# Seven products in place of eight in two stages of a chain of matrix products on one core

## The chip, the core and the metric

The kernel runs on one core of a Trainium2 chip. The time is that of one execution on the device, in us; less is better.

## What is computed

Three stages follow each other, all in float32 at the borders. Attention with a decay makes `x` (1536 tokens by 512), a gated product of two linear maps makes `y`, and a softmax-like stage with a normalisation makes the output:

```python
attn_out = _attn_ref(**attn_kwargs)                  # 16 heads, 12 blocks of 128 here, a carried state
x = np.ascontiguousarray(attn_out.transpose(0, 2, 1, 3)).reshape(B * S, H * D)
...
a = x @ w_a                                          # 1536 x 512 by 512 x 1536
b = x @ w_b
x = (a * b @ w_out).astype(np.float32)               # by 1536 x 512
...
h = x @ w_in                                         # 1536 x 512 by 512 x 1024
h_max = np.max(h, axis=-1, keepdims=True)
e = np.exp(h - h_max)
sm = e / (np.sum(e, axis=-1, keepdims=True) + 1e-09)
solu = h * sm
mu = np.mean(solu, axis=-1, keepdims=True)
var = np.mean((solu - mu) ** 2, axis=-1, keepdims=True)
ln = (solu - mu) / np.sqrt(var + 1e-06) * g_ln
return (ln @ w_out).astype(np.float32)               # by 1024 x 512
```

## The kernel before

Each factor of a large product is scaled by a power of two and split into a high and a low half in float16; `mm3` then makes each product of two tiles from three matmuls (high by high, high by low, low by high), accumulated in one PSUM bank of 512 float32 columns. There are eight banks, taken by `bank`.

The tokens are worked in 12 chunks `n` of 128 (two batches in turn, six blocks each) and in three groups `t` of 512. For each chunk, `scores`, `products` and `carry` do the attention in float32 with small matmuls, `kdecay`, `qdecay` and `fade` prepare operands on GpSimd; `scale_x` finds a scale and `split_x` writes the two halves of `x`. Weights come in as 1 MB pieces: `load_w` on the DMA queue of SP, `decode` (two ScalarE passes, a VectorE shift, a maximum), `scale_w` (through `spread` and `pow2`, which send a maximum over partitions through TensorE), `split_w`.

`L1(t, f)` makes 128 rows of `a` and of `b` for a group `t`: 12 matmuls each into `pa` and `pb`, then ScalarE copies `pa`, VectorE multiplies by `pb`, ScalarE casts to the high half and GpSimd subtracts for the low one (`g`). `f` runs over 12 blocks, so there are 36 calls. `L2(t, d)` multiplies by `w_out` over all 12 `f` in four quarters of 12 matmuls; `scale_y` and `split_y` split `y`. `L3(t, j)` makes `h` of one chunk in two banks `ph` (24 matmuls of 512 columns) and carries on to the softmax and the normalisation; `Z` splits and transposes the result, `L4` is the last product and sends it out.

All these are generators. ORDER is a list of words such as `L,0,3`, written out by hand or by a planner: each word runs its generator up to its next `yield`, so ORDER alone sets the order of instructions on every engine's queue, each of which works in order. SBUF tiles come from fixed numbers of buffers by kind (`BUFS`: 6, 11, 18 of 4 KB a partition, 3 of 8 KB, and others); a tile waits until an earlier one of its kind is released. The constants `lam`, `dec` and `gl` are loaded from GpSimd's queue at the start.

Of the kernel before, what the change touches and what calls it, by code (L numbers as in the profile page):

```python
# [587 lines left out]
```

## Time and profile before

| | us |
|---|---|
| median of three runs (lowest to highest) | 474.37 (473.40 to 475.82) |
| the profiled execution | 473.23 |
| its span | 471.5 |
| TensorE busy with matmuls | 455.6 (2682 of them) |
| weight loads, beside the matmuls | 230.8 |
| VectorE busy | 281.3 |
| ScalarE busy | 185.1 |
| GpSimd busy | 125.2 |

Busy time counts every us in which an engine has an instruction in work. The profile names the engines PE (TensorE; PEld its weight loads), DVE (VectorE), ACT (ScalarE), POOL (GpSimd) and SP (the one that issues DMA). Matmul records overlap, so the cost of one in a stream is its distance from the next, not its duration. A number after L is a line of the kernel before.

### The profile page before, as it was taken

Reading aid. Unit: us, or ns where it says so; the run is one execution under the profiler, and the core shown is the slowest. Engines: PE = TensorE matmul, PEld = TensorE weight load, DVE = VectorE, ACT = ScalarE, POOL = GpSimd, SP = SyncE. Lnnn points to the kernel's source line nnn. Section 1 sums busy time; section 2 is a strip of 40 time slices with the busy share of each in tenths; the row PEclk is TensorE's granted clock in tenths of the full one; section 3 lists DMA queues with packets and bytes.
Section 4 is the critical chain, followed back from the end, with each engine's and each line's share of the span. In section 5 each row is a group of like instructions: output and inputs, shape, how many; then the busy total and the mean of one; then the engine's idle time right before and its main releaser. Section 6 shows DMA issues by size and latency. Waiting matters only on the chain.

```text
span 471.5 us, 6724 instructions
## 1 busy us (share of the span) xinstructions
PE 455.6 (97%) x2682; PEld 230.8 (49%) x2682; DVE 281.3 (60%) x529; ACT 185.1 (39%) x289; POOL 125.2 (27%) x183
## 2 busy tenths in 40 slices
PE   3899999999999999999999999999999999999997
...
GB/s 272 414 207 181 267 180 0 2 91 245 201 188 179 170 178 90 178 89 91 1 2 89 90 0 0 1 0 1 45 2 22 23 111 83 74 128 30 68 89 46
DMA packets 30320, 48.69 MB, mean 103 GB/s; under 512 B 22224, under 2 KB 22480, under 8 KB 26960
## 3 DMA queue, kind: packets, MB, share of 16 engines
...
## 4 chain that ended last, share of the span: by engine, by line
PE 87%; DVE 8%; DMA 2%; issue 1%; POOL 1%; ACT 0%; DVEq 0%; POOLq 0%
PE py L128 20%; PE pb L128 18%; PE pa L128 17%; PE po L128 13%; PE ph L128 13%; PE px L225 2%; DMA dec<-in_dec_dram 2%; DVE fab L289 2%; PE pss L204 2%; DVE st_ab L102 1%; PE px L220 1%; DVE sc L209 1%; DVE xh L267 1%; DVE wab L343 1%; DVE xst L102 1%
## 5 line engine op out<-in xcount | busy, mean ns | idle before, releaser
L128 PEld LDWEIGHTS <-wab 128*128 128x128 f16 x888 | 85.7, 98 | 98.5 <-DVE wab L343 1.3
L128 PE MATMUL pa<-xh,wab 128*128 128x512 f16 (+1 forms) x444 | 98.5, 373 | 1.1 <-DVE wab L343 0.8
L373 POOL TENSOR_TENSOR g<-asb,g 128x512 f16<-128x512 f32 x36 | 46.7, 1310 | 196.9 <-ACT g L371 196.8
L128 PE MATMUL pb<-xh,wab 128*128 128x512 f16 (+1 forms) x444 | 98.4, 373 | 0.0
L128 PE MATMUL py<-g,wo 128*128 128x512 f16 x432 | 94.3, 379 | 0.0
L128 PEld LDWEIGHTS <-wo 128*128 128x128 f16 x432 | 42.2, 98 | 50.6
L366 DVE TENSOR_TENSOR asb<-asb,pb 128x512 f32<-128x512 f32 x36 | 24.4, 684 | 67.2 <-PE pb L128 62.8
L128 PE MATMUL po<-wo,zT 128*128 128x512 f16 (+1 forms) x312 | 63.4, 363 | 0.0
L128 PE MATMUL ph<-wi,yh 128*128 128x512 f16 x288 | 63.4, 379 | 0.0
L128 PEld LDWEIGHTS <-zT 128*128 128x128 f16 x312 | 30.5, 98 | 31.5
L128 PEld LDWEIGHTS <-yh 128*128 128x128 f16 x288 | 28.1, 98 | 33.7
L364 ACT ACTIVATE asb<-pa 128x512 f32<-128x512 f32 x36 | 20.8, 590 | 53.2 <-PE pa L128 48.8
L371 ACT CAST g<-asb 128x512 f16<-128x512 f32 x36 | 21.3, 614 | 26.5 <-DVE asb L366 26.5
L287 ACT ACTIVATE raw<-raw 128x1024 f32<-128x1024 f32 x26 | 29.5, 1136 | 0.0
L477 POOL TENSOR_TENSOR zr<-e,zr 128x512 f16<-128x512 f32 x20 | 22.7, 1156 | 23.0 <-ACT zr L473 23.0
L102 DVE TENSOR_REDUCE ym<-py 128x1 f32<-128x512 f32 x12 | 8.3, 691 | 31.4 <-PE py L128 31.3
L437 ACT ACTIVATE e<-ph,st,ch 128x512 f32<-128x512 f32 x24 | 18.4, 776 | 19.0 <-DVE st L432 13.7
L518 ACT ACTIVATE ob<-po,glm 128x512 f32<-128x512 f32 (+1 forms) x13 | 8.5, 655 | 41.7 <-PE po L128 41.7
L430 DVE TENSOR_REDUCE st<-ph 128x1 f32<-128x512 f32 x24 | 15.9, 674 | 12.9 <-PE ph L128 12.8
L473 ACT CAST zr<-e 128x512 f16<-128x512 f32 x20 | 11.4, 618 | 28.0 <-DVE e L462 28.0
L204 PE MATMUL pss<-qk 64*128 64x128 f32 x192 | 15.3, 308 | 7.1 <-DMA qk<-in_qk_dram 7.1
L340 ACT ACTIVATE wab<-fab,sab 128x512 f16<-128x512 f32 x24 | 15.9, 714 | 16.0 <-DVE sab L122 15.7
(109 smaller groups left out, 462.9 us busy)
## 6 DMA issues: line engine op xcount, KB each, us to landing
...
zT<-zr SPq DMA_TRANSPOSE x20, 3.1
...
```

The costliest lines, as they stand in the source:

```text
L102: nc.vector.tensor_reduce(out=dst, in_=src, axis=AX.X, op=ALU.max, apply_absolute_value=True)
L128: nc.tensor.matmul(o, w[a], x[b], start=start and i == 0, stop=stop and i == 2, skip_group_check=True)
L204: nc.tensor.matmul(pss[e][:, a * P:(a + 1) * P], t[r, 1, a], t[r, 0, a], start=True, stop=True, skip_group_check=True)
L287: nc.scalar.activation(hi.bitcast(F32), hi.bitcast(F32), AF.Prelu, scale=2.0 ** -112, alpha=2.0 ** 32)
L340: nc.scalar.activation(w[:, z, 0], src[:, z], AF.Copy, scale=s)
L364: nc.scalar.activation(a, pp[0], AF.Copy, scale=2.0 ** -63)
L366: nc.vector.tensor_mul(a, a, pp[1])
L371: nc.scalar.copy(g[:, 0], a)
L373: nc.gpsimd.tensor_sub(g[:, 1], a, g[:, 0])
L430: nc.vector.tensor_reduce(out=st[:, z:z + 1], in_=ph[z], axis=AX.X, op=ALU.max)
L437: nc.scalar.activation(e[z], ph[z], AF.Exp, bias=st[:, 2:3], scale=c, accum_out=st[:, 3 + z:4 + z])
L477: nc.gpsimd.tensor_sub(lo, e[z], hi)
```

## The change

Two products are made by a scheme of Strassen's kind (Winograd's form, with seven block products and fifteen sums in place of eight block products):

- `x w_a` and `x w_b` for pairs 2 to 5 of the blocks `f` and all three groups `t`: `R1(t, p)` takes the place of two `L1`. The blocks are two halves of the 512 inputs, two blocks `f`, and two halves of the 512 tokens, so its matmuls have 256 columns. Pairs 0 and 1 stay with `L1`.
- `y w_in` for all chunks: `L3(t, i)` makes two chunks at once, with matmuls of 512 columns. What followed in `L3` is now `norm(t, j)`; for the even chunk it works on 1024 columns in SBUF at once.

The sums of blocks are made by `sums_x`, `sums_w`, `sums_y`, `sums_i`, and split into halves by `sums_x` itself, `split_s`, `split_ys`, `split_si`. Weights `a` and `b` share one scale for two `f`; scales leave two more bits of room (TOP). `pow2` keeps its maximum in PSUM and the reciprocal of a scale is taken later (`turn`). One kind of 41 buffers takes the place of four kinds, `lam`, `dec` and `gl` are loaded from ScalarE's queue, and ORDER is written anew (1322 words in place of 1050).

```diff
-ORDER = ("G,qk,0 G,kv,0 G,qk,1 G,ab,0 G,kv,1 G,qk,2 G,kv,2 G,qk,3 G,kv,3 G,ab,1 G,qk,4 G,kv,4 G,qk,5 G,kv,5 A,0 K,0 A,1 K,0 A,0 T,0 A,1 T,0 A,1 O,2 A,0 D,ab,0 "
+ORDER = ("G,qk,0 G,qk,1 G,qk,6 G,kv,0 G,kv,1 G,qk,3 G,qk,2 G,ab,2 G,kv,3 G,ab,1 G,kv,2 G,kv,4 G,kv,7 G,qk,5 A,0 A,1 A,0 A,0 Q,6 A,6 A,1 K,0 C,0 A,1 K,0 A,6 C,1 "
...
-BUFS = {"in": 6, "w": 11, "g": 18, "xy": 3, "raw": 2, "row": 8}
+PLAIN, PLAINW = [0, 1, 2], [0, 1]
+TOP = 12
+BUFS = {"k": 41, "raw": 2, "row": 8}
...
-        m = sm.tile([P, n], F32, name=f"m{n}")
+        m = pm[:, n * P:n * P + n]
...
-    nc.gpsimd.dma_start(out=lam8, in_=lam)
+    nc.scalar.dma_start(out=lam8, in_=lam)
     dec = const.tile([P, NP, P], F32, name="dec")
-    nc.gpsimd.dma_start(out=dec[:, :, 0:1], in_=dec0)
+    nc.scalar.dma_start(out=dec[:, :, 0:1], in_=dec0)
...
+    def sums_x(m):
+        t, i = m // 2, m % 2
+        s1, s2 = sx[m][:, 0, :1], sx[m][:, 0, 1:]
+        o1, o2 = (px[n].rearrange("p (a i) -> p a i", a=NP) for n in (2 * m, 2 * m + 1))
+        b12 = t_row("b12", (P, 2, P))
+        tt = t_k("tt", (P, 4, 2, P))
+        nc.scalar.activation(b12, o2[:, :2], AF.Copy, scale=s2)
+        yield
+        for k, (a, s, op, b) in enumerate(((o1[:, :2], s1, ALU.subtract, b12), (o2[:, 2:], s2, ALU.add, tt[:, 0]), (o2[:, 2:], s2, ALU.subtract, b12), (o1[:, 2:], s1, ALU.subtract, tt[:, 1]))):
+            nc.vector.scalar_tensor_tensor(out=tt[:, k], in0=a, scalar=s, in1=b, op0=ALU.mult, op1=op)
+            yield
+        if t not in xt:
+            xt[t] = [t_k("xt", (P, 2, 2, W), F16) for _ in range(2)]
+        hl = [[xt[t][k][:, :, z].rearrange("p a (q i c) -> p q a i c", q=2, i=2)[:, :, :, i] for z in range(2)] for k in range(2)]
+        for k in range(2):
+            nc.scalar.copy(hl[k][0], tt[:, 2 * k:2 * k + 2])
+            yield
+        for k in range(2):
+            nc.gpsimd.tensor_sub(hl[k][1], tt[:, 2 * k:2 * k + 2], hl[k][0])
...
+    def sums_w(p):
+        def w(e, k):
+            return fw["ab", 2 * p + e][:, :, k * W // 2:(k + 1) * W // 2]
+        fs[p] = [t_k("s12", (P, 2, W))]
+        u = [fs[p][0][:, :, k * W // 2:(k + 1) * W // 2] for k in range(2)]
+        nc.gpsimd.tensor_add(u[0], w(1, 0), w(1, 1))
+        yield
+        nc.gpsimd.tensor_sub(u[1], u[0], w(0, 0))
+        yield
+        fs[p].append(t_k("s34", (P, 2, W)))
+        v = [fs[p][1][:, :, k * W // 2:(k + 1) * W // 2] for k in range(2)]
+        nc.gpsimd.tensor_sub(v[0], w(0, 0), w(1, 0))
+        yield
+        nc.gpsimd.tensor_sub(v[1], u[1], w(0, 1))
...
+    def split_s(p, k):
+        src = fs[p][k]
+        w = wt["s", p, k] = t_k("ws", (P, 2, 2, W), F16)
+        ss = sab[:, 0, p]
+        for z in range(2):
+            nc.scalar.activation(w[:, z, 0], src[:, z], AF.Copy, scale=ss[:, z:z + 1])
...
+    def R1(t, p):
+        x = xs[t]
+        H = W // 2
+        f, h = (lambda z, e=e: wt["ab", 4 * p + 2 * e + z] for e in range(2))
+        u, v = (lambda z, k=k: wt["s", p, k][:, z] for k in range(2))
+        def product(o, w, k, x, i, start, stop):
+            for z in range(2):
+                for kk in range(2):
+                    ks = slice((2 * k + kk) * P, (2 * k + kk + 1) * P)
+                    mm3(o[:, z], (w(z)[:, 0, ks], w(z)[:, 1, ks]), (x[:, kk, 0, i * H:(i + 1) * H], x[:, kk, 1, i * H:(i + 1) * H]), start and z == 0 and kk == 0, stop and z == 1 and kk == 1)
+        def acc(nm):
+            return bank(nm).rearrange("p (z n) -> p z n", z=2)
+        def kept(nm, o):
+            r = t_row(nm, (P, 2, H))
+            nc.scalar.activation(r, o, AF.Copy, scale=2.0 ** -28)
+            return r
+        A, Bk = acc("rA"), acc("rB")
+        product(A, f, 0, x[0], 0, True, False)
+        yield
+        product(Bk, u, 0, xt[t][0], 0, True, False)
+        yield
+        p1 = kept("p1", A)
+        yield
+        product(A, u, 1, xt[t][0], 1, False, False)
+        yield
+        p5 = kept("p5", Bk)
+        yield
+        product(Bk, v, 1, x[1], 1, False, True)
+        yield
+        p16 = kept("p16", A)
+        yield
+        product(A, v, 0, xt[t][1], 0, False, False)
+        yield
+        c0 = t_k("c0", (P, 2, 2, H))
+        nc.vector.scalar_tensor_tensor(out=c0[:, 1], in0=Bk, scalar=-2.0 ** -28, in1=p16, op0=ALU.mult, op1=ALU.add)
+        yield
+        C = acc("rC")
+        product(C, f, 1, x[1], 0, True, True)
+        yield
+        p167 = kept("p167", A)
+        yield
+        product(A, h, 1, xt[t][1], 1, False, True)
+        yield
+        nc.vector.scalar_tensor_tensor(out=c0[:, 0], in0=C, scalar=2.0 ** -28, in1=p1, op0=ALU.mult, op1=ALU.add)
+        yield
+        c1 = t_k("c1", (P, 2, 2, H))
+        nc.gpsimd.tensor_sub(c1[:, 1], p167, p5)
+        yield
+        nc.scalar.activation(c1[:, 0], A, AF.Copy, scale=2.0 ** -28)
+        yield
+        for c in (c0, c1):
+            nc.vector.scalar_tensor_tensor(out=c[:, :, 0], in0=c[:, :, 0], scalar=2.0, in1=c[:, :, 1], op0=ALU.mult, op1=ALU.mult)
+            yield
+        for e, c in enumerate((c0, c1)):
+            g = pair(t, p)[:, e].rearrange("p z (q n) -> p z q n", q=2)
+            nc.scalar.copy(g[:, 0], c[:, :, 0])
+            yield
+            nc.gpsimd.tensor_sub(g[:, 1], c[:, :, 0], g[:, 0])
...
-        return halve(pys.pop((t, d)), sy[t][:, 0], ys[t][:, d])
+        f = yf[t][d // 2][:, d % 2]
+        nc.scalar.activation(f, pys.pop((t, d)), AF.Copy, scale=sy[t][:, 0])
+        yield
+        if t not in ys:
+            ys[t] = [t_k("yh", (P, 2, 2, W), F16) for _ in range(2)]
+        c = slice(0, W if d // 2 else W // 2)
+        y = ys[t][d // 2][:, d % 2]
+        nc.scalar.copy(y[:, 0, c], f[:, c])
+        yield
+        nc.gpsimd.tensor_sub(y[:, 1, c], f[:, c], y[:, 0, c])
...
+    def sums_y(t):
+        (y11, y21), (y12, y22) = (halves(yf[t][h]) for h in range(2))
+        yfs[t] = [t_k("yu", (P, 2, W))]
+        u = halves(yfs[t][0])
+        nc.gpsimd.tensor_add(u[0], y21, y22)
+        yield
+        nc.gpsimd.tensor_sub(u[1], u[0], y11)
+        yield
+        yfs[t].append(t_k("yv", (P, 2, W)))
+        v = halves(yfs[t][1])
+        nc.gpsimd.tensor_sub(v[0], y11, y21)
+        yield
+        nc.gpsimd.tensor_sub(v[1], u[1], y12)
...
+    def split_ys(t, k):
+        src = yfs[t][k]
+        if t not in yt:
+            yt[t] = {}
+        y = yt[t][k] = t_k("yt", (P, 2, 2, W), F16)
+        nc.scalar.copy(y[:, :, 0], src)
+        yield
+        nc.vector.tensor_sub(y[:, :, 1], src, y[:, :, 0])
...
+                nc.gpsimd.tensor_sub(ifs[0][:, r], w(0, 0), w(0, 1))
+            elif k == 1:
+                nc.gpsimd.tensor_add(ifs[1][:, r], w(1, 1), ifs[0][:, r])
+            elif k == 2:
+                nc.gpsimd.tensor_sub(ifs[2][:, r], w(1, 1), w(0, 1))
+            else:
+                nc.gpsimd.tensor_sub(ifs[3][:, r], w(1, 0), ifs[1][:, r])
...
+    def L3(t, i):
         y = ys[t]
+        at = [slice(place(t, 2 * i + e) * P, (place(t, 2 * i + e) + 1) * P) for e in range(2)]
+        ss = [slice(k * W // 2 + i * P, k * W // 2 + (i + 1) * P) for k in range(2)]
+        def product(o, y, c, w, start, stop):
+            for r in range(2):
+                wh, wl = w(r)
+                mm3(o, (y[:, r, 0, c], y[:, r, 1, c]), (wh, wl), start and r == 0, stop and r == 1)
+        def wi(h, z):
+            return lambda r: (wt["i", 2 * (2 * h + r) + z][:, 0], wt["i", 2 * (2 * h + r) + z][:, 1])
+        def si(k):
+            return lambda r: (wt["si", k][:, r, 0], wt["si", k][:, r, 1])
+        def kept(nm, o):
+            r = t_row(nm, (P, W))
+            nc.scalar.copy(r, o)
+            return r
+        A, Bk = bank("hA"), bank("hB")
+        product(A, y[0], at[0], wi(0, 0), True, False)
+        yield
+        product(Bk, yt[t][0], ss[0], si(0), True, False)
+        yield
+        p1 = kept("p1", A)
+        yield
+        product(A, yt[t][0], ss[1], si(1), False, False)
+        yield
+        p5 = kept("p5", Bk)
+        yield
+        product(Bk, yt[t][1], ss[1], wi(1, 1), False, True)
+        yield
+        p16 = kept("p16", A)
+        yield
+        product(A, yt[t][1], ss[0], si(2), False, False)
+        yield
+        h = t_k("h", (P, 2, W))
+        nc.vector.tensor_sub(h[:, 1], p16, Bk)
+        yield
+        C = bank("hC")
+        product(C, y[1], at[0], wi(1, 0), True, True)
+        yield
+        p167 = kept("p167", A)
+        yield
+        product(A, y[1], at[1], si(3), False, True)
+        yield
+        nc.vector.tensor_add(h[:, 0], p1, C)
+        hs[t, 2 * i] = h
+        yield
+        r = t_row("h22", (P, W))
+        nc.gpsimd.tensor_sub(r, p167, p5)
+        hs[t, 2 * i + 1] = (A, r)
```


In ORDER, `R` is `R1`, `J`, `H`, `B` and `I` are the sums of x, w, y and w_in, `E`, `F` and `k` their splits, `N` is the new `L3` and `n` is `norm`.

## Rows read from the trace of the kernel before

**Rows 1.** by stretch: us, busy us and count on PE, PEld, DVE, ACT, POOL; clock, DMA share, GB/s

```profile
0.00:34.56 34.56, 24.04 (x326) 20.59 (x327) 22.33 (x45) 11.64 (x16) 22.68 (x40) 1.00 0.81 305
...
34.56:80.00 45.44, 43.62 (x364) 25.11 (x364) 43.66 (x73) 20.99 (x30) 17.49 (x16) 1.00 0.42 163
...
80.00:468.00 388.00, 387.98 (x1995) 185.05 (x1992) 215.26 (x412) 152.01 (x244) 85.04 (x127) 1.00 0.25 79
```

**Rows 2.** groups of TensorE's instructions: busy us, mean ns | idle before

```profile
L128 PE MATMUL pb<-xh,wab 128*128 128x512 f16 x420 | 95.5, 379 | 0.0
...
L128 PE MATMUL ph<-wi,yh 128*128 128x512 f16 x288 | 63.4, 379 | 0.0
...
L128 PE MATMUL po<-wo,zT 128*128 128x256 f16 x48 | 5.4, 273 | 0.0
...
L128 PEld LDWEIGHTS <-wab 128*128 128x128 f16 x888 | 85.7, 98 | 98.5 <-DVE wab L343 1.3 <-issue 1.0
```

**Rows 3.** TensorE in order of time: start us, us, what, count [idle before <-releaser]

```profile
446.16 10.52 PE L128 MATMUL po<-wo,zT 128*128 128x512 f16 x48
...
457.39 10.58 PE L128 MATMUL po<-wo,zT 128*128 128x512 f16 x72
```

**Rows 4.** groups of ScalarE's and VectorE's instructions, columns as in rows 2

```profile
L364 ACT ACTIVATE asb<-pa 128x512 f32<-128x512 f32 x36 | 20.8, 590 | 53.2 <-PE pa L128 48.8 <-POOL g L373 4.5
...
L371 ACT CAST g<-asb 128x512 f16<-128x512 f32 x36 | 21.3, 614 | 26.5 <-DVE asb L366 26.5
...
L340 ACT ACTIVATE wab<-fab,sab 128x512 f16<-128x512 f32 x24 | 15.9, 714 | 16.0 <-DVE sab L122 15.7 <-DVE wab L343 0.2
...
L283 ACT ACTIVATE fab<-raw 128x1024 uint32<-128x1024 uint16 x12 | 13.8, 1152 | 5.1 <-DMA raw<-in_wab_dram 5.1
...
L366 DVE TENSOR_TENSOR asb<-asb,pb 128x512 f32<-128x512 f32 x36 | 24.4, 684 | 67.2 <-PE pb L128 62.8 <-PE pm L111 4.4
...
L445 DVE SCALAR_TENSOR_TENSOR e<-e,st,ph 128x512 f32<-128x512 f32 x24 | 17.0, 744 | 0.5
...
L289 DVE SCALAR_TENSOR_TENSOR fab<-raw,fab 128x1024 uint32<-128x1024 uint32 x12 | 16.1, 1353 | 2.6 <-ACT raw L287 2.6
...
L102 DVE TENSOR_REDUCE st_ab<-fab 128x2 f32<-128x1024 f32 x12 | 14.5, 1215 | 0.2
...
L250 DVE TENSOR_TENSOR state<-old,pst 128x256 f32<-128x256 f32 x8 | 3.2, 410 | 0.1
```

**Rows 5.** VectorE, GpSimd and TensorE in order of time, the first 14 us

```profile
6.76 2.63 DVE L172 TENSOR_TENSOR_SCAN mask<-lam,ident 128x128 f32<-128x128 f32 x8 [2.55 <-DMA lam<-in_lam_dram]
...
10.06 2.63 POOL L175 TENSOR_TENSOR dec<-dec 128x4 f32<-128x4 f32 x7 [6.11 <-DMA dec<-in_dec_dram]
...
13.32 1.59 PE L244 MATMUL pst<-kv,kd 128*64 128x64 f32 x15 [2.04 <-POOL kd L189]
```

**Rows 6.** all engines around 60 us, then single lines: ns min/median/max

```profile
59.90 2.62 POOL L189 TENSOR_TENSOR kd<-kv,mask 128x256 f32<-128x256 f32 x2
...
60.94 2.13 DVE L343 SCALAR_TENSOR_TENSOR wab<-fab,sab,wab 128x512 f16<-128x512 f32 x2
...
62.10 0.39 PE L128 MATMUL pa<-xh,wab 128*128 128x512 f16 x1 [0.85 <-DVE wab L343]
...
L343 DVE SCALAR_TENSOR_TENSOR wab<-fab,sab,wab x24: 731/747/1815, 33.4 to 173.2; 128x512 f16<-128x512 f32 x24
...
L373 POOL TENSOR_TENSOR g<-asb,g x36: 1147/1159/2133, 67.5 to 313.2; 128x512 f16<-128x512 f32 x36
...
L195 POOL TENSOR_TENSOR qd<-qk,dec x10: 1257/1275/2183, 17.3 to 104.5; 128x512 f32<-128x512 f32 x10
...
L189 POOL TENSOR_TENSOR kd<-kv,mask x20: 613/620/1639, 12.7 to 61.5; 128x256 f32<-128x256 f32 x20
```

**Rows 7.** TensorE and VectorE around 443 us, in order of time

```profile
442.69 2.75 PE L128 MATMUL ph<-wi,yh 128*128 128x512 f16 x12
...
445.49 0.69 DVE L430 TENSOR_REDUCE st<-ph 128x1 f32<-128x512 f32 x1 [1.93 <-PE ph L128]
```

More of the change, by code (lines that the diff above doesn't have):

```diff
@@ L252, in carry, with place @@
         yield
+    def place(t, j):
+        return (j % 2) * 2 + j // 2
     def scale_x(m):
         sx[m] = const.tile([P, 2, 2], F32, name=f"sx{m}")
-        return pow2(xst[m], 2, sx[m])
+        return pow2(xst[m], 2, sx[m], TOP)
     def split_x(n):
@@ L260, in split_x @@
         if t not in xs:
-            xs[t] = t_xy("xh", (P, KD, 2, W), F16)
+            xs[t] = [t_k("xh", (P, 2, 2, W), F16) for _ in range(2)]
         s = sx[n // 2][:, 0, n % 2:n % 2 + 1]
         o = px[n].rearrange("p (a i) -> p a i", a=NP)
-        xh, xl = (xs[t][:, :, z, j * P:(j + 1) * P] for z in range(2))
-        nc.scalar.activation(xh, o, AF.Copy, scale=s)
+        c = slice(place(t, j) * P, (place(t, j) + 1) * P)
+        hs = [1] if j % 2 and t not in PLAIN else [0, 1]
+        for h in hs:
+            nc.scalar.activation(xs[t][h][:, :, 0, c], o[:, 2 * h:2 * h + 2], AF.Copy, scale=s)
@@ L304, in scale_w @@
         s = scl[nm] = const.tile([P, 2, 1], F32, name="s" + nm)
-        yield from pow2(r, 1, s)
+        yield from pow2(r, 1, s, TOP if nm == "i" else 14)
+        turn(s)
         if nm == "o2":
@@ L348, in body, with pair @@
     gts = {t: {} for t in range(NB)}
+    def pair(t, p):
+        if p not in gts[t]:
+            gts[t][p] = t_k("g", (P, 2, 2, W), F16)
+            for e in range(2):
+                gs[t][2 * p + e] = gts[t][p][:, e]
+        return gts[t][p]
     def L1(t, f):
@@ L352, in L1, with rows @@
         pp = [bank("pa"), bank("pb")]
-        parts = [(0, W // 2), (W // 2, W)] if (t, f) in HALVED else [(0, W)]
-        for c0, c1 in parts:
-            c = slice(c0, c1)
+        for i in ((0, 1) if (t, f) in HALVED else (slice(0, 2),)):
+            def rows(a):
+                a = a.rearrange("p (q i c) -> p q i c", q=2, i=2)
+                return a[:, :, i]
             for z in range(2):
@@ L396, in scale_y @@
         s = sy[t] = const.tile([P, 2, 1], F32, name=f"sy{t}")
-        ys[t] = t_xy("yh", (P, KD, 2, W), F16)
-        yield from pow2(r, 1, s)
+        yield from pow2(r, 1, s, TOP)
         yield
+        turn(s)
+        for m in range(2 * t, 2 * t + 2):
+            turn(sx[m])
         c = sm.tile([P, 1], F32, name="c")
@@ new lines, in body, with halves @@
+    yfs, yt = {}, {}
+    def halves(x):
+        return [x[..., k * (W // 2):(k + 1) * (W // 2)] for k in range(2)]
+    def sums_y(t):
[12 more added lines that the diff above has]
+        yield
@@ L434, in L3 @@
-        e2 = t_in("e", (P, 2, W))
+        h = hs[t, j]
+        whole = j % 2 == 0
+        zs_ = [slice(0, 2)] if whole else [0, 1]
+        src = [h] if whole else h
+        for z, x in enumerate(src):
+            if whole:
+                x = x.rearrange("p z n -> p (z n)")
+            nc.vector.tensor_reduce(out=st[:, z:z + 1], in_=x, axis=AX.X, op=ALU.max)
+            if z == len(src) - 1:
+                nc.vector.tensor_scalar(st[:, 2:3], st[:, 0:1], st[:, z:z + 1], cn, op0=ALU.max, op1=ALU.mult)
+            yield
@@ L435, in L3 @@
+        e2 = t_k("e", (P, 2, W))
         e = [e2[:, z] for z in range(2)]
-        for z in range(2):
-            nc.scalar.activation(e[z], ph[z], AF.Exp, bias=st[:, 2:3], scale=c, accum_out=st[:, 3 + z:4 + z])
+        for z, x in zip(zs_, src):
+            k = 0 if whole else z
+            nc.scalar.activation(e2[:, z], x, AF.Exp, bias=st[:, 2:3], scale=c, accum_out=st[:, 3 + k:4 + k])
         yield
-        nc.vector.scalar_tensor_tensor(out=st[:, 5:6], in0=st[:, 3:4], scalar=1e-9, in1=st[:, 4:5], op0=ALU.add, op1=ALU.add)
+        if whole:
+            nc.vector.tensor_scalar(st[:, 5:6], st[:, 3:4], 1e-9, None, op0=ALU.add)
+        else:
+            nc.vector.scalar_tensor_tensor(out=st[:, 5:6], in0=st[:, 3:4], scalar=1e-9, in1=st[:, 4:5], op0=ALU.add, op1=ALU.add)
@@ L460, in L3 @@
         yield
-        for z in range(2):
-            nc.vector.tensor_scalar(e[z], e[z], st[:, 8:9], r, op0=ALU.subtract, op1=ALU.mult)
-            if z == 1:
+        for z in [slice(0, 2)] if whole else range(2):
+            nc.vector.tensor_scalar(e2[:, z], e2[:, z], st[:, 8:9], r, op0=ALU.subtract, op1=ALU.mult)
+            if whole or z == 1:
                 es[t, j] = e
@@ L533, in body @@
     kinds = {"G": load, "A": scores, "K": kdecay, "Q": qdecay, "C": products, "O": fade, "T": carry, "X": scale_x, "Y": split_x,
-             "D": decode, "P": scale_w, "S": split_w, "L": L1, "M": L2, "U": scale_y, "V": split_y, "N": L3, "Z": Z, "W": L4}
+             "D": decode, "P": scale_w, "S": split_w, "J": sums_x, "H": sums_w, "E": split_s, "R": R1, "L": L1, "M": L2, "U": scale_y, "V": split_y, "B": sums_y, "F": split_ys, "I": sums_i, "k": split_si, "N": L3, "n": norm, "Z": Z, "W": L4}
     parts = {}
```

139 lines of the change are left out of this document (88 added, 51 removed), and 91 rows, old and new, of the table ORDER.

## The prediction

> **What bounds the kernel now.** I read the busy times by stretch first, then the matmul groups, then the order of events on each engine. TensorE is the bound, at full granted clock: 387.98 of the 388 us from 80 to 468 us are matmul time. It is idle for 10.5 us before the first product of `L1` at 34.56 us, 1.8 us from there to 80 us, and 3.5 us at the end [rows 1]. That is 15.8 of the span of 471.5 us. Before 80 us VectorE is the tight one: 43.66 of 45.44 us [rows 1].
>
> A busy matmul record overlaps its neighbour, so I take spacings. 48 matmuls of 512 columns run in 10.52 us and the last lasts 0.379, so (10.52 - 0.379)/47 = 0.2158 us each. The final stretch holds 24 of them and 48 of 256 columns; (10.58 - 0.273 - 24 x 0.2158)/47 = 0.1091 us for 256 columns [rows 2, 3]. So a half-width matmul costs 1.01 halves, although every matmul loads its own weights (98 ns a load, under 109) [rows 2]. The saving rests on that.
>
> **Matmuls.** A pair of `f` for one `t` takes 2 x 24 matmuls of 512 columns, 10.36 us. `R1` takes 7 products of 12 with 256 columns: 84 x 0.1091 = 9.16 us. ORDER calls it for pairs 2 to 5 and three `t`: 12 x 1.19 = 14.3 us. Two chunks of `y w_in` take 48 x 0.2158; the new `L3` takes 7 x 6 = 42, so 1.29 us less, six times: 7.8 us. The weights of a and b get one scale for two `f`, which leaves out 12 small matmuls of 128 columns, at a quarter of 0.2158 some 0.6 us. Sum: 22.7 us off TensorE. With nothing else changed the profiled 473.2 us (span 471.5 and 1.7 around it) become 450.5.
>
> **Work put on the other engines.** For each pair `R1` has on ScalarE five PSUM copies and two casts, 5 x 0.59 + 2 x 0.61 = 4.2 us, against 2.4 for two `L1`; on VectorE four operations at 0.744, 3.0 against 1.4; on GpSimd three of 1.16 to 1.28, 3.6 against 2.3 [rows 4, 6]. Twelve times that is +21, +19 and +15 us. `sums_w` adds 16 GpSimd sums of 1.28 us (20 us), `split_s` 16 casts and 16 subtractions (11 and 12 us), `sums_x` six times 1.6 us of ScalarE, 4 x 0.41 of VectorE and 2.3 of GpSimd (10, 10, 14 us). At w_in the copies, sums and splits (`kept`, `sums_y`, `split_ys`, `sums_i`, `split_si`) are about +28 of ScalarE, +10 of VectorE, +44 of GpSimd. Halved splits, one wide operation in place of two and fewer scales give some 10 to 15 us back on ScalarE and VectorE. Before, they were busy 185, 281 and 125 us; they come to about 260, 325 and 215, all far under TensorE's 433. `pow2` leaves its maximum in the PSUM bank and puts the reciprocal off (`turn`): a few operations of tenths of a us, which I cost at nothing. So none becomes the bound of the whole; each must be looked at by stretch.
>
> **The start.** Counting ORDER's steps up to the first product of `L1`, VectorE has 10.1 us more to do: eight operations of `sums_x` (3.3), two more decode shifts and one more maximum (3.6), two more mask multiplies (1.4), one more split of a weight (0.7), `split_x` in halves (1.1), a state sum (0.4), less 0.4 of scales [rows 4]. TensorE gets 1.2 us more before that point. VectorE was busy 22.33 of the 34.56 us and idle 12.2 [rows 1]. Part of this idleness goes: the mask scan waited 2.55 us for lam, GpSimd 6.11 us for dec, kd and then the state product 2.04 us behind that [rows 5]; the change issues lam and dec from ScalarE's queue, with no data queued ahead there, and puts the scores of two more chunks and `px` of chunk 0 in front of the state products. I let idleness fall to 7.3 us: 22.3 + 10.1 + 7.3 = 39.7 us, of which TensorE works 24.0 + 1.2, so it idles 14.5 in place of 10.5: +4. If nothing of the wait goes, 44.6 us and +9; if it falls to 3.3, which leaves little but the wait for the first data, 0. The row nearest to the middle is lam's 2.55 with about half of the waits on kd. ORDER also moves loads: SP still issues the same 50 weight and input transfers, and before the first `L1` some 11 MB must land, 36 us at the 305 GB/s of the stretch up to 34.56 [rows 1]; so DMA is nearly as tight as VectorE, and shortening one further wouldn't bring a gain alone. The 1.8 us of stalls up to 80 us I leave.
>
> **The hand-overs inside a round.** Each `R1` and each new `L3` accumulates several products in one bank, and ScalarE must copy a partial sum before the product after next may add to it (`kept`): four such waits in a round, 72 in all. The wait is new on TensorE, whose queue is in order: all later matmuls, those of `L2` and `L4` too, stand behind it. A product lasts 12 x 0.1091 = 1.31 us (6 x 0.2158 = 1.29). The copy needs 0.16 us until the last matmul is out (0.273 - 0.109), 0.05 to be seen by the next engine [rows 7], 0.59, and about 0.05 back: 0.85 us. So a lone round runs without a stall with 0.44 us to spare if ScalarE is free. If ScalarE has just begun a decode pass of 1.15 us [rows 4], 0.71 us are lost; if the other round or an `L1` is put in between, nothing. The steps of two rounds are interleaved in most of ORDER. I take 2 us in all (three such hits), with bounds 0 and 10.
>
> **What is hidden.** From the last product of `t` = 0 in `L2` to the first `L3` ORDER has twelve quarters of `L2`, 12 x 2.59 = 31 us of matmuls, over a chain of scale, split, four GpSimd sums and a split of about 10 us. For `t` = 2 there are some 14 us over the same chain, mostly two `L4` of 5.2; without them up to 10 us would show. After the last `L3` come more than 40 us of `L4`, longer than any softmax chain, and the last output leaves as before: 3.5 us. The 41 common buffers hold as much as the four kinds before (6 + 11 + 18 + 3 x 2), so transfers don't come free earlier; I cost this at nothing.
>
> **A rule against the change.** At 60 us a pair of GpSimd's and a pair of VectorE's with two SBUF operands take turns: 2.62 us where two of the median 620 ns take 1.2, and 2.13 where two of 747 ns take 1.5, and TensorE stalls 0.85 us for the result. The longest of each kind are twice the median or more: 1815 ns against 747, 2133 against 1159 [rows 6]. The Trainium skill, SBUF — State Buffer, section Who interferes with whom, says why: a VectorE operation with two SBUF inputs and a GpSimd operation that reads SBUF hold the same port exclusively, and whoever starts first blocks the other wholly. The trace agrees in those numbers. By the sum above the forecast assumes that order hides it; by that rule taken strictly the next rival holds.
>
> **Rivals.** (a) The two engines become one. In the 41.2 us of matmuls at 62 to 103 us of TensorE's work (from the end of the plain `L1` to the middle of the first rounds) GpSimd has 24 operations, 29.4 us, and VectorE 23 with two SBUF operands, 17.0 us: 46.4, so 5.2 us over. At the sums and splits of `y` and w_in (272 to 294) 15.5 and 11.5, 27.0 stand against 22.1: 4.9 more. All of it on the path gives 456.5 + 10.1 = 466.6 us, half of it 461.6. For it: the 0.85 us stall now, where the two engines have less to do. Against: the stretches around are slack. (b) Start and rounds cost nothing: 450.5. For it: nothing but VectorE and data holds TensorE up at the start, and both begin earlier. (c) The half-width matmuls don't save, because TensorE waits for weights: at 0.131 us each (132.1 us of 612 full ones over 1008) the gain in `R1` and `L3` together is gone: 450.5 + 22 + 2 = 475. Against it: weight loads are 98 ns, and 48 such matmuls ran at 0.1091 [rows 2, 3]. (d) Slower: hand-overs find ScalarE taken. At 165 to 207 us of TensorE's work ScalarE has 39 us to do in 42 us of matmuls, twelve decode passes of 1.15 us among it. If half of the 72 lose 0.71 us, 25.6 us: 473.2 - 22.7 + 4 + 25.6 = 480. It decides from a mean loss of about 0.3 us for a hand-over (72 x 0.3 = 21.6). Against it: interleaving, and TensorE's 0.02 us of idle in 388 us under the present order [rows 1], where `pa` and `pb` also pass through ScalarE, though two banks later.
>
> **How the numbers follow.** 473.2 - 22.7 + 4 + 2 = 456.5. The median of the runs, 474.37, is 1.1 above the profiled time, inside their spread. Chances: the forecast with its own bounds (453 to 461) 0.55; (b) 0.15; (a) 0.20; (c) 0.04; (d) 0.06. From 450 to 468 takes in the first three but for their tails. A measurement of this kernel can tell about 0.5%, 2.4 us, from no change. Faster 0.90, the same 0.04, slower 0.06.
>
> **What would show it.** In the profile of the changed kernel: matmul time near 433 us; 12 products of 256 columns spaced at 0.109; first `L1` product near 40 us with TensorE idle some 14 us before; idle after 80 us of a few us in all, put down to ScalarE's `kept` copies; longest records of VectorE's two-operand steps and GpSimd's sums near 2 us around 80 to 110 us. The forecast is wrong if spacing passes 0.115, if waits on `kept` sum to over 10 us, or if the first `L1` product comes after 45 us or before 36.

## The result, and the profile after

The changed kernel takes 467.1 us (median of 4 runs, 465.76 to 469.55) against 474.35 us of the kernel before beside it: a ratio of 0.985, 95% interval 0.9802 to 0.9899. That is 7.25 us of gain where 17.9 were forecast for the median (16.7 from the profiled times). The time is near that of rival (a), 466.6 us; how far that is luck stands below. The profiled execution took 467.45 us, span 465.6 (before 473.2 and 471.5).

By stretch, columns as in [rows 1]:

```profile
0.00:40.00 40.00, 26.17 (x352) 22.21 (x354) 31.08 (x62) 18.20 (x29) 25.71 (x40) 0.90 0.81 310
40.00:80.00 40.00, 40.00 (x369) 25.36 (x366) 33.99 (x60) 21.52 (x36) 23.02 (x24) 0.97 0.50 189
...
100.00:107.00 7.00, 4.76 (x42) 3.55 (x39) 7.00 (x5) 2.28 (x4) 5.84 (x4) 1.00 0.08 33
107.00:300.00 193.00, 193.00 (x1446) 136.36 (x1444) 142.34 (x206) 125.92 (x190) 83.89 (x62) 1.00 0.21 77
300.00:316.00 16.00, 8.36 (x29) 3.02 (x28) 15.69 (x26) 6.49 (x10) 10.44 (x6) 0.68 0.00 1
```

TensorE is busy 438.5 us in all, not the 432.9 that the forecast comes to. Read the first and the eighth column: the time is lost in three places. Up to 80 us it is idle for 13.8 us (before: 10.5 + 1.8, [rows 1]) and its clock is no longer 1.00. At 100 to 107 us it is idle for 2.2. At 300 to 316 us it is idle for 7.6, and at a low clock after that. In between, 193 us without a gap: the rounds themselves run as they should.

TensorE's waits (waited for: us, times, longest):

```profile
PE pss L218 <- DMA qk<-in_qk_dram: 6.8, 4, 4.4
PE pm L122 <- DVE ry L113: 5.6, 1, 5.6
PE rB L142 <- DVE ws L441: 2.2, 3, 0.8
...
PE hA L142 <- DVE wi L400: 2.0, 1, 2.0
```

Two waits, for the clamp scale of `y` (`ry`, the power of two found from its maximum) and the split of w_in (`wi`), make the 7.6 us; `ws`, the split of the sums of w_ab, makes the 2.2. All three come from VectorE. No line names ScalarE's `kept` copies. In order of time, VectorE, GpSimd and TensorE around the two places (start us, us, what):

```profile
99.62 6.77 DVE L441 SCALAR_TENSOR_TENSOR ws<-s,sab,ws 128x512 f16<-128x512 f32 x4
...
286.67 5.98 DVE L410 SCALAR_TENSOR_TENSOR wo<-fo,glm,wo 128x512 f16<-128x512 f32 x4
...
296.56 1.27 DVE L661 SCALAR_TENSOR_TENSOR wsi<-si,wsi 128x1024 f16<-128x1024 f32 x1
...
298.36 1.69 DVE L633 TENSOR_TENSOR yt<-yu,yt 128x1024 f16<-128x1024 f32 x1
...
300.57 3.89 DVE L400 SCALAR_TENSOR_TENSOR wi<-fi,si,wi 128x1024 f16<-128x1024 f32 x2
304.38 2.28 DVE L661 SCALAR_TENSOR_TENSOR wsi<-si,wsi 128x1024 f16<-128x1024 f32 x1
306.59 4.26 DVE L400 SCALAR_TENSOR_TENSOR wi<-fi,si,wi 128x1024 f16<-128x1024 f32 x2
...
100.78 1.71 POOL L424 TENSOR_TENSOR s<-s,fab 128x512 f32<-128x512 f32 x1
102.45 1.71 POOL L428 TENSOR_TENSOR s<-fab 128x512 f32<-128x512 f32 x1
...
298.93 4.45 POOL L652 TENSOR_TENSOR si<-fi,si 128x512 f32<-128x512 f32 x2
303.34 2.24 POOL L650 TENSOR_TENSOR si<-fi 128x512 f32<-128x512 f32 x1
305.55 4.23 POOL L601 TENSOR_TENSOR yh<-yf,yh 128x512 f16<-128x512 f32 x2
...
304.51 1.58 PE L142 MATMUL hA<-wi,yh 128*128 128x512 f16 x5 [2.03 <-DVE wi L400]
311.70 0.29 PE L122 MATMUL pm<-identb,ry 128*128 128x128 bf16 x1 [5.61 <-DVE ry L113]
311.78 2.77 PE L142 MATMUL hB<-wsi,yt 128*128 128x512 f16 x6
```

Four splits take 6.77 us where four of [rows 6]'s median, 747 ns, take 3.0; GpSimd's sums beside them take 1.71 us each where 1.25 is usual. The two engines go in step, as in [rows 6], only for longer. VectorE works almost without a gap from 283 to 311 us (27.9 of 28) and so `ry` comes at 311.6. This `ry` belongs to the next group, `t` = 1. In ORDER its words `U,1` stand between the first and the second product of `N,0,0`, so one small matmul holds up `hB`, both of whose factors are written by 300.1 us (`wsi` and `yt` above) and which starts 0.1 us behind it. No run moved these words, so what that place in ORDER costs by itself is not known. VectorE's groups (busy us, mean ns):

```profile
L441 DVE SCALAR_TENSOR_TENSOR ws<-s,sab,ws 128x512 f16<-128x512 f32 x16 | 15.3, 998 | 0.2 <-ACT ws L438 0.2
L410 DVE SCALAR_TENSOR_TENSOR wo<-fo,glm,wo 128x512 f16<-128x512 f32 x8 | 12.7, 1630 | 0.0
...
L400 DVE SCALAR_TENSOR_TENSOR wi<-fi,si,wi 128x1024 f16<-128x1024 f32 x4 | 8.2, 2078 | 0.0
```

### The profile page after: what moved, and what is told of

It reads as the page before. It is cut to its first block, busy times and chain, and to the rows that moved or that the text cites. A ratio compares the mean times of both kernels' runs of the same rounds, so it can differ in the third digit from the quotient of the medians.

```text
span 465.6 us, 7745 instructions
## 1 busy us (share of the span) xinstructions
PE 438.5 (94%) x3066; PEld 270.3 (58%) x3066; DVE 350.4 (75%) x564; ACT 249.1 (53%) x395; POOL 238.8 (51%) x258
## 4 chain that ended last, share of the span: by engine, by line
PE 79%; DVE 10%; POOL 7%; DMA 2%; ACT 1%; issue 1%; ACTq 0%; POOLq 0%
PE py L142 15%; PE rA L142 13%; PE po L142 11%; PE pa L142 6%; PE rB L142 6%; PE pb L142 6%; PE hA L142 6%; PE rC L142 3%; PE hB L142 3%; DVE wo L410 3%; PE px L239 2%; PE px L233 2%; DVE wi L400 2%; PE hC L142 2%; DMA dec<-in_dec_dram 2%; POOL kd L203 1%
## 5 line engine op out<-in xcount | busy, mean ns | idle before, releaser
L142 PEld LDWEIGHTS <-wo 128*128 128x128 f16 x432 | 42.2, 98 | 50.2
L142 PEld LDWEIGHTS <-ws 128*128 128x128 f16 x576 | 56.0, 98 | 9.9 <-DVE ws L441 3.1
L545 POOL TENSOR_TENSOR g<-c,g 128x512 f16<-128x512 f32 x24 | 31.4, 1326 | 31.8 <-ACT g L543 31.7
L142 PE MATMUL rA<-xt,ws 128*128 128x256 f16 x288 | 35.2, 273 | 0.0
L142 PE MATMUL pa<-xh,wab 128*128 128x512 f16 (+1 forms) x156 | 33.9, 369 | 0.0
L534 POOL TENSOR_TENSOR c<-p,p 128x512 f32<-128x512 f32 x12 | 17.8, 1485 | 30.2 <-ACT p L501 24.0
L142 PE MATMUL pb<-xh,wab 128*128 128x512 f16 (+1 forms) x156 | 33.2, 363 | 0.0
L501 ACT ACTIVATE p<-rA 128x512 f32<-128x512 f32 x36 | 21.4, 597 | 16.5 <-PE rA L142 16.1
L142 PEld LDWEIGHTS <-yt 128*128 128x128 f16 x144 | 14.5, 101 | 18.2 <-issue 2.5
L410 DVE SCALAR_TENSOR_TENSOR wab<-fab,sab,wab 128x512 f16<-128x512 f32 (+1 forms) x24 | 21.8, 935 | 1.5 <-ACT wab L407 1.5
L539 DVE SCALAR_TENSOR_TENSOR c<-c 128x512 f32<-128x512 f32 x24 | 19.7, 844 | 4.2 <-POOL c L534 3.4
L478 POOL TENSOR_TENSOR g<-asb,g 128x512 f16<-128x512 f32 x12 | 15.0, 1254 | 14.5 <-ACT g L476 14.5
```

The costliest lines, as they stand in the source:

```text
L142: nc.tensor.matmul(o, w[a], x[b], start=start and i == 0, stop=stop and i == 2, skip_group_check=True)
L410: nc.vector.scalar_tensor_tensor(out=w[:, z, 1, c], in0=src[:, z, c], scalar=ss[:, z:z + 1], in1=w[:, z, 0, c], op0=ALU.mult, op1=ALU.subt ...
L478: nc.gpsimd.tensor_sub(g[:, 1], a, g[:, 0])
L501: nc.scalar.activation(r, o, AF.Copy, scale=2.0 ** -28)
L534: nc.gpsimd.tensor_sub(c1[:, 1], p167, p5)
L539: nc.vector.scalar_tensor_tensor(out=c[:, :, 0], in0=c[:, :, 0], scalar=2.0, in1=c[:, :, 1], op0=ALU.mult, op1=ALU.mult)
```

## The experiments

Theories on the two later places: T1, VectorE's steps with two SBUF operands and GpSimd's steps that read SBUF take turns; T2, VectorE simply has too much to do there; T3, the hand-overs of rounds. On the start: S1, GpSimd's queue; S2, the loads' order on SyncE; S3, the constants' move to ScalarE's queue. In the expectations S1 also takes in VectorE's steps before the first product. Every time stands with its ratio to runs of the kernel before on the same chip.

**Which half.** One half alone, the other by plain products. First y w_in alone by seven products (pairs of `x w_a` by `L1`; the words J, H and E left out of ORDER):

```diff
-PLAIN, PLAINW = [0, 1, 2], [0, 1]
+PLAIN, PLAINW = [0, 1, 2], [0, 1, 2, 3, 4, 5]
```

> Seven products for y w_in alone: every pair of f goes back to plain products, and the sums of x and of w_a, w_b with their splits are left out. TensorE gets 12 x 1.19 = 14.3 us of matmuls back. Theory 1 (the losses are two places where VectorE and GpSimd block each other, 100 to 107 and 300 to 316 us, and a start held up by the sums of x on GpSimd): the stall near 100 us (2.2) goes, most of the start's loss goes (some 5 us), the stall near 305 us stays at about 9: 467 + 14 - 2 - 5 = 474 us, level with the kernel before. Theory 2 (VectorE simply has too many operations in these places, GpSimd has no part): the same sign, as the operations go too. Theory 3 (the hand-overs of partial sums inside a round cost the missing time): 72 hand-overs become 24, so 11 of the missing 17 us come back: 467 + 14 - 11 = 470 us with the start unchanged.

Measured: 480.11 us, 1.0124 (1.0094 to 1.0154), slower than before. The waits on `ry` (5.9) and `wi` (2.0) are there as in the changed kernel, and the first product of `L1` starts at 42.2 us although the sums of `x` are gone. Both numbers were missed: the stall stayed, as T1 has it, but the start gave nothing back, and T1's sum without that gain is 479. T3's 470 is farther off, and TensorE waits for no `kept` copy in the changed kernel: T3 falls. Then x w_a and x w_b alone:

> Seven products for x w_a and x w_b alone: y w_in goes back to plain products (two chunks at once, 48 matmuls), its sums and their splits are left out, split_y makes both halves of all of y. TensorE gets 6 x 1.29 = 7.8 us of matmuls back. Theory 1: the stall of 7.6 us near 305 us and the slower clock behind it (1.8) go or shrink to 2 at most: 467 + 8 - 8 = 467 us, so the whole second half of the change is worth nothing as it stands. Theory 2: much the same, 467 to 469. Theory 3 (hand-overs): 48 of 72 hand-overs stay and the gain of 7.8 is lost: 473 to 475.

Measured: 463.67 us, 0.9799 (0.9743 to 0.9854), 3 us under T1's number, while T3 had 473 to 475. TensorE has no gap at 280 to 320 us. So the w_in half, whose matmuls are 7.8 us less, gives nothing as it stands (by the two ratios 2.4 us slower with it, within the intervals): it brings its own stall.

**GpSimd's reads.** The eight sums of w_in's chunks replaced by two fills each, which write the same tiles and read nothing:

```diff
-                nc.gpsimd.tensor_sub(ifs[0][:, r], w(0, 0), w(0, 1))
+                [nc.gpsimd.memset(ifs[0][:, r], 0.5 + n) for n in range(2)]
```

> The eight sums of w_in on GpSimd are each replaced by two fills of the same tile (so w_in's sums are not computed): GpSimd writes, and is busy for about as long, but reads nothing. VectorE's and ScalarE's operations are unchanged. Theory 1 in its sharp form (an operation of GpSimd that reads SBUF holds what VectorE needs for its second SBUF operand): the eight operations of w_out (1630 ns) and four of w_in (2078 ns) come down towards 750 and 1300 ns, 8 us at least, and the stall of 7.6 us near 305 us goes to under 2: 458 to 460 us. Theory 2: nothing changes, 467. If GpSimd's queue itself is what is late, 467 too, unless fills are shorter than sums.

Measured: 458.17 us, 0.9656 (0.9634 to 0.9678); the kernel leaves the sums of w_in out. VectorE has the same steps:

```profile
L410 DVE SCALAR_TENSOR_TENSOR wo<-fo,glm,wo 128x512 f16<-128x512 f32 x8 | 7.2, 945 | 0.0
L400 DVE SCALAR_TENSOR_TENSOR wi<-fi,si,wi 128x1024 f16<-128x1024 f32 x4 | 6.3, 1601 | 0.0
```

The means fell from 1630 and 2078 ns, and of the 7.6 us of idle time 1.8 are left. The means mix three cases. The first five splits of w_out (739 to 745 ns) start with GpSimd idle, not beside fills; the longest of both groups (1766 and 2174 ns) lie beside the sums and low halves of `y`, which still read. What fills do is seen in a split that lies beside them from start to end:

```profile
296.94 2.16 POOL L652 MEMSET si<- 128x512 f32 x4
...
298.15 1.27 DVE L661 SCALAR_TENSOR_TENSOR wsi<-si,wsi 128x1024 f16<-128x1024 f32 x1
...
299.04 1.11 POOL L650 MEMSET si<- 128x512 f32 x2
```

It takes 1.27 us, as such a split does with GpSimd idle in the next run (1.27), where one beside GpSimd steps that read took 2.28 in the changed kernel (at 304.38 us). VectorE was given no less to do, so T2 falls and T1 holds. GpSimd itself has less to do (13.8 us of 280 to 300 in place of 17.2), so the 458 us hold that gain too; the durations are the test. By the Trainium skill, SBUF — State Buffer, section Who interferes with whom, a VectorE instruction with two SBUF inputs contends with a GpSimd instruction that reads SBUF, not with one that only writes it; the trace agrees, with 2.28 us beside steps that read and 1.27 beside fills.

**The same sums on VectorE.** All twenty sums of `y` and w_in moved from GpSimd to VectorE:

```diff
-        nc.gpsimd.tensor_add(u[0], y21, y22)
+        nc.vector.tensor_add(u[0], y21, y22)
```

> The twenty sums of y and w_in go from GpSimd to VectorE, all else as in the changed kernel. Between 282 and 311 us that puts 12 more operations on VectorE, of about 0.6 us each (512 columns, both operands in SBUF), 7 us. Theory 1: there VectorE's own operations are stretched by about 11 us in all (eight of w_out by 0.9, four of w_in by 0.8 each), and most of that goes, as the sums no longer block it: stall and clock about as now or a little less, 464 to 468 us. Theory 2: VectorE, full from 282 to 311 us, falls 7 us further behind: 473 to 475 us.

Measured: 464.85 us, 0.9798 (0.9769 to 0.9827). VectorE was given twenty steps of 680 ns more, 13.6 us, and the kernel isn't slower for it, let alone at T2's 473 to 475: T2 falls again.

```profile
L410 DVE SCALAR_TENSOR_TENSOR wo<-fo,glm,wo 128x512 f16<-128x512 f32 x8 | 7.4, 959 | 0.0
...
L400 DVE SCALAR_TENSOR_TENSOR wi<-fi,si,wi 128x1024 f16<-128x1024 f32 x4 | 5.1, 1270 | 0.0
```

The splits gave back 5.3 and 3.1 us, and the twelve of these sums that lie there took most of it; `ry` is still waited for, 5.0 us.

**The second w_out later.** The 16 words `S,o2,*` spread behind the first product of w_in:

> The sixteen steps of split_w for the last weights (eight of VectorE's two-operand operations, eight casts) leave the stretch from 281 to 297 us and stand, spread out, between the first L3 and the first L4, which is the first to need them. Nothing else moves. Theories 1 and 2 both let the stall near 305 us shrink: with 13 us of VectorE's time gone there (eight of 1630 ns) it goes, and so does the slow clock behind it: 457 to 459 us. If the stall is set by the chain from y alone (scale, split, sums, split), it stays: 466.

Measured: 463.36 us, 0.9798 (0.9739 to 0.9858); `ry` 3.2 us: between the two expectations. Each of these edits alone mends a part: from 280 to 320 us TensorE is idle for 6.1 us with the sums on VectorE and for 3.2 with the late splits, against 7.6. Either the sums or the splits are then still in the same 28 us; with both edits, below, 2.6 are left at most.

**The place at 101 us.** GpSimd's last three sums of pair 4 and two `qd` moved some words later in ORDER, behind the splits of pair 5's sums:

> Around 97 to 107 us four splits of sums of weights on VectorE (ws) take 1.7 us each while GpSimd runs two qd and three sums for the next pair; here these five stand behind the four splits. VectorE's work is untouched. Theory 1: the four run at 750 ns, TensorE's three waits for them (2.2 us) go to under 0.5: 464 to 465 us. Theory 2 (VectorE too full): 467, with the waits as now.

Measured: 466.2 us, 0.9842 (0.981 to 0.9875), the four splits again 6.77 us. GpSimd had nothing to wait for ahead of the moved steps, so they ran at the same time, 95.4 to 103.8 us, in another order: no test. Placed behind a step that itself has to wait, the low half of `g`:

> Against the changed kernel's 467.1: the last three sums of pair 4 now stand behind the first low half of g on GpSimd's queue, and the two qd behind the second; both wait for ScalarE until about 110 us, so that GpSimd has nothing to do under the splits of pair 5's sums (before this edit it works without a break at 91 to 106). T1 (the shared port): the four splits that took 6.77 us take 3.0 to 3.5 (near 750 to 870 ns each), TensorE's wait there of 2.2 us at 101 to 107 goes to under 0.5, median 464.5 to 465.5. T2 (VectorE is too full): the splits still take 1.5 us and more each, wait and time unchanged. If the c on GpSimd at 111.5, now 4 us later, is what TensorE needs next, a wait shows at 112 to 125 and the time stays.

Measured: 470.16 us, 0.9913 (0.9883 to 0.9942). The splits (first line), then ScalarE and TensorE 25 us later:

```profile
98.21 2.73 DVE L441 SCALAR_TENSOR_TENSOR ws<-s,sab,ws 128x512 f16<-128x512 f32 x4
...
123.69 0.62 ACT L543 CAST g<-c 128x512 f16<-128x512 f32 x1 [5.50 <-DVE c L539]
...
124.85 2.72 PE L142 MATMUL rA<-xt,ws 128*128 128x256 f16 x12 [3.99 <-ACT p L501]
```

2.73 us in place of 6.77, and the wait for `ws` is gone: T1. But GpSimd's moved steps now stand ahead of the `c` of a round, which comes 3 us later against TensorE's products; ScalarE's cast of it waits 5.5 us, the next copy of a partial product stands behind that cast, and TensorE waits 4.0 us for the bank: the forecast's hand-over stall, made by hand. With that edit, the sums on VectorE and the late w_out together:

> Three edits at once: the sums of y and w_in on VectorE, the second w_out's splits after the first w_in products, and the edit of the run beside it. T1: the w_out splits no longer meet GpSimd, the wait for ry and wi at 300 to 312 us falls from 7.6 to under 1.5, that at 101 to 107 to under 0.5, and the clock stays 1.00 at 280 to 320: 6 + 2 + up to 1.5 less than 467.1, 458 to 460. T2: VectorE, which takes 13 us more of work in the stretch 250 to 310, is late with what the w_in products want: 465 or more.

Measured: 463.82 us, 0.9779 (0.9751 to 0.9808), not the 458 to 460 of T1, with the 4.0 us still in it. Then the repair: pair 4's last three sums on VectorE behind the splits of pair 5's sums, the two `qd` behind the splits of pair 4.

```diff
+        eng = nc.vector if p == 4 else nc.gpsimd
-        nc.gpsimd.tensor_sub(u[1], u[0], w(0, 0))
+        eng.tensor_sub(u[1], u[0], w(0, 0))
```

> As the three edits together (463.8 us), but the last three sums of pair 4 are made by VectorE behind its splits, and the two qd stand later on GpSimd's queue, so that the c, on which ScalarE's next copy of a product and TensorE's bank wait, isn't held up at 112 us. T1: splits there at 680 to 750 ns, no wait at 101 to 107, none at 120 to 125 (there 4.0 us), all else as in the three together: 463.8 less 4, 459 to 461. If VectorE's 2 us of sums more are in the way instead, a wait on ws or wab at 103 to 115 takes up to 2 of it: 461 to 462.

Measured: **457.8 us, 0.9642 (0.9618 to 0.9667)**, the fastest kernel of this study, 9.3 us under the changed one and a little under the expected 459 to 461. By stretch, and the group of the splits:

```profile
100.00:107.00 7.00, 7.00 (x67) 6.29 (x66) 6.08 (x12) 3.59 (x7) 0.89 (x1) 1.00 0.00 0
300.00:316.00 16.00, 14.59 (x68) 6.30 (x66) 15.48 (x40) 9.90 (x17) 4.21 (x5) 1.00 0.01 2
```

```profile
L442 DVE SCALAR_TENSOR_TENSOR ws<-s,sab,ws 128x512 f16<-128x512 f32 x16 | 11.2, 743 | 0.2 <-ACT ws L439 0.2
```

VectorE makes 23 sums more than in the changed kernel and is busy for less: 345.7 us in place of 350.4. GpSimd is busy for 201.4 in place of 238.8.

**The start.** The low halves of the sums of `x` put behind the first product (S1):

> In the changed kernel GpSimd works without a break from 9 to 36 us, and 5.5 us of that are four subtractions of sums_x that nothing needs before about 100 us. Here they stand in ORDER behind the first product of L1 has been made. If GpSimd's queue sets the start (theory S1), the state products come earlier and the first product of L1 starts near 36 us in place of 41, total 462 to 464 us. If the loads set it (theory S2: the inputs of chunk 4 land at 34.6 us, behind weights for which SP waits), the first product stays within 1 us of 41 and the total at 466 to 467.

Measured: 468.8 us, 0.9899 (0.9865 to 0.9934), first product at 41.3: S1 falls as far as it is GpSimd's queue. The constants again from GpSimd's queue, as in the kernel before (S3):

> lam, dec and gl are loaded from GpSimd's queue again, one part of the change undone. In the changed kernel SP's waits name the landing of lam, dec and gl (1.5, 3.8 and 0.9 us), and SP issues nothing between 4.5 and 10 us but two loads. If moving them brought that wait (theory S3), SP's issues of 4.5 to 13 us come 4 us earlier here, GpSimd's and VectorE's waits for kv go, and the first product of L1 comes 1 to 2 us earlier, although the mask scan starts 2.2 us later again: 465 to 466 us. If the move was a gain by the earlier mask alone, the start is 2 us longer: 469.

Measured: 468.02 us, 0.9897 (0.9862 to 0.9931). SyncE issues five loads between 3.1 and 5.5 us where the changed kernel, in which the profile has it wait for lam and dec, issues two between 4.5 and 10; yet chunk 4's q and k still leave at 27.1, behind two loads that wait for a buffer, and the first product starts at 40.3. S3 thus has at most 0.8 us of the start and none of the time. So that load ahead of the two as well (S2):

```diff
-G,ab,0 G,ab,9 G,qk,4
+G,qk,4 G,ab,0 G,ab,9
```

> The constants from GpSimd's queue, and the load of chunk 4's q and k ahead of the two loads of w_ab that wait until 24.6 us for a buffer. S2 (the loads' order on SyncE sets the start): chunk 4's scores start at 28 to 32 instead of 34.7, the first product of x w_a at 36 to 38.5 instead of 41.1, and the mean clock of the first 40 us rises over 0.93: 2 to 4 us less, 463 to 465. S1 (the chain of decode, clamp scale and the splits of x on VectorE and GpSimd sets it): scores start earlier, the product still at 40 to 41.5, time 466.5 to 468.

Measured: 467.38 us, 0.9848 (0.982 to 0.9877). The first product comes at 40.3, not at 36 to 38.5, so S2 alone falls too. The load is in time, and TensorE waits for the next thing:

```profile
33.96 1.16 PE L218 MATMUL pss<-qk 64*128 64x128 f32 x16
36.49 1.09 PE L233 MATMUL px<-qd,state 64*64 64x128 f32 x16 [1.37 <-POOL qd L209]
...
39.33 1.09 PE L239 MATMUL px<-sc,kv 128*64 128x128 f32 x14 [1.16 <-DVE sc L223]
40.34 1.48 PE L142 MATMUL pa<-xh,wab 128*128 128x256 f16 x12
```

Beside the three later edits it brings nothing either:

> The edits of the two runs beside it together. If the losses are separate places that add up: the time of the three edits together less what the start's edit gave, 455 to 458 where S2 holds, 458 to 460 where it doesn't. If what one place gives back is waited for at the next, no better than the three together.

Measured: 463.74 us, 0.9776 (0.974 to 0.9812), against 463.82 without it. Without the sums of `x`:

> The kernel with plain products for x w_a and x w_b (no sums of x before the first product; 480.1 us, first product of x w_a at 42.2) with the two edits of the loads (constants from GpSimd's queue, chunk 4's q and k ahead of the two loads of w_ab). S2b (the start has two limits that end within 2 us of each other: the load of chunk 4's q and k, and VectorE, which before the first product also makes the sums of x, 8 times 477 ns = 3.8 us): with both away the first product starts at 36 to 38, the clock stays above 0.95 at 20 to 40, time 476 to 478. If neither is a limit (a third, such as the third decode of 1.6 to 1.9 us and its maximum of 1.2 us on VectorE): 40 to 42 as before, time 479.5 to 480.5.

Measured: 478.67 us, 1.0089 (1.0074 to 1.0104); first product at 39.6, between the two expectations. Its wait is `pm L119 <- DVE r L110` of 2.4 us: the clamp scale of weights 0 and 1, of which 0 is loaded third, through two buffers. Loading and decoding 0 first:

> As the kernel of 457.8 us (sums on VectorE, second w_out late, GpSimd's work out from under the splits at 101), with the two edits of the loads, and with the weights 0 and 1 of w_ab, which the first product needs, loaded and decoded first, 2 third (before: 2, 1, 0, so that 0 waited for one of the two buffers of encoded weights until 24.7 us and was decoded at 33); their clamp scale ahead of the third decode. S4 (the third load through two buffers sets the start): clamp scale ready by 33 to 35, first product of x w_a at 37 to 39 instead of 41, clock above 0.9 at 20 to 40, time 455 to 456.5. If VectorE's queue (scores, splits and sums of x: 18.2 of 20 us busy) holds it in any case: first product at 40 to 41, time 457.5 to 458.

Measured: 460.36 us, 0.9702 (0.968 to 0.9725), slower than the 457.8 it started from. VectorE, then TensorE:

```profile
36.29 1.23 DVE L341 SCALAR_TENSOR_TENSOR fab<-raw,fab 128x1024 uint32<-128x1024 uint32 x1 [0.23 <-ACT raw L339]
37.55 1.22 DVE L113 TENSOR_REDUCE st_ab<-fab 128x2 f32<-128x1024 f32 x1
38.68 1.28 DVE L223 TENSOR_TENSOR sc<-pss,mask 128x512 f32<-128x512 f32 x2
...
39.41 2.57 PE L239 MATMUL px<-sc,kv 128*64 128x128 f32 x16 [2.55 <-DVE sc L223]
41.92 2.74 PE L142 MATMUL pa<-xh,wab 128*128 128x256 f16 x12
```

The clamp scale is ready at 35.1 us (38.7 in the run with the early load), but chunk 4's scores now stand behind the third decode on VectorE, and its products stand ahead of `L1` on TensorE. As I read these traces, three chains (chunk 4's load and scores, the weights' clamp scale, the sums and splits of `x`) end within 4 us of each other, all through VectorE. It is busy for 18.2 to 18.6 of the 20 us from 20 to 40 in most of these kernels, but a full VectorE alone does not set the start: with y w_in alone and with the late low halves it was busy for 14.5 and 16.1, and the product came at 42.2 and 41.3. None of these runs brought the first product ahead of 39 us (before: 34.56); how it could be is left open.

## Why the prediction was wrong

**Matmuls: right.** Twelve products of 256 columns run in 1.31 us as put, and the 193 us without a gap at 107 to 300 show it. The 5.6 us by which TensorE is busy for longer than forecast are put down to the clock, below (4.1 + 2.2).

**Hand-overs: +2 put, 0 came.** No wait on `kept`. The bound was not empty: the run with three sums ahead of `c` shows one of 4.0 us.

**Start: +4 put, about 5.6 came, otherwise than put.** The first product came at 41.1 us, not 39.7. VectorE's work up to it was sized well (32.2 us, put 32.4), its idle time too low (8.9, put 7.3). TensorE was idle for 13.8 us before it, put 14.5, and the stalls of 1.8 us up to 80, which the forecast left, are gone: its idle time up to 80 us grew by 1.5 (13.8 against 12.3). The rest is the clock. Two stretches before, and the same two after:

```profile
20.00:25.00 5.00, 5.00 (x92) 4.36 (x93) 4.90 (x11) 3.39 (x4) 5.00 (x8) 1.00 1.04 418
25.00:30.00 5.00, 4.92 (x82) 4.09 (x78) 4.89 (x9) 0.00 (x0) 4.67 (x7) 1.00 0.86 347
...
20.00:25.00 5.00, 2.74 (x52) 2.30 (x48) 4.34 (x9) 4.92 (x6) 3.44 (x4) 1.00 0.84 334
25.00:30.00 5.00, 3.02 (x28) 2.50 (x30) 4.83 (x10) 2.44 (x7) 5.00 (x6) 0.54 0.89 315
```

After these gaps the clock falls to its lower level (0.5, 1.2 of 2.4 GHz) for a part of the time. Five groups of matmuls between 27 and 43 us then take 4.1 us longer than the same shapes at full clock (16 state products 1.70 against 0.69, 16 scores 2.08 against 1.16, and so on). The forecast counted gaps as lost time and not that they can slow what follows. The 4.1 us are a count of busy time, not what the clock cost: three of the five groups (2.6 us) stand ahead of a wait for chunk 4's q and k, which at full clock would have been longer. Why the first product comes late stays open.

**What is hidden: here the forecast failed.** The step that failed is "order hides it", which put the two engines' taking turns at nothing and made it rival (a) with a chance of 0.20. It costs 2.2 us at 101 and 7.6 at 302 to 312, and there too the clock falls: 0.53 and 0.50 in the ten us from 305, three groups of matmuls 2.2 us longer than at full clock (six at 311.78 take 2.77 us where 5 x 0.2158 + 0.379 = 1.46 is usual). Together 12.0 us, of which the runs with the sums and splits moved got most back; rival (a) had 5.2 + 4.9 = 10.1, at these two places, the first too dear by 3, the second too cheap by 5. The second was too cheap because only the sums and splits of `y` and w_in stood in it; the eight splits of the second w_out lie in the same 28 us and were stretched too, from 0.74 to 1.63 us each. That rival (a)'s 466.6 us is so near is partly luck: start +1.6, hand-overs -2, the two places -3 and +5 against its terms.

The argument "against" was that the stretches around are slack. At 80 to 107 us and behind 283 they are so for TensorE's next products, not for VectorE: from 283 on its queue is full to the last us once its steps take twice their time. "What is hidden" followed the chains of `t` = 0 and `t` = 2; the longest wait, 5.6 us, was for the scale of `t` = 1. For the whole kernel the forecast came to about 325 us of VectorE and 215 of GpSimd; 350.4 and 238.8 came. And the longest records of [rows 6] are not all "twice the median or more": 2133 against 1159 ns is 1.8 times. The check that would have told: sum VectorE's and GpSimd's reading steps not over 40 us of matmuls but from the first data of a chain to the product that needs it, with all that ORDER puts on VectorE in between.

**The sum with what came.** -22.7 + 5.6 (start) + 0 (hand-overs) + 2.2 + 9.8 = -5.1 us, against -5.9 between the spans. The 0.8 us between them aren't explained; the two counts of clock come to 0.7 more than the 5.6 us of busy time. With both late places mended the kernel takes 457.8 us, near the forecast's 456.5; of the waits at w_in 2.6 us are left in it.
